# Softmax-factored linear attention into a multiplicative FFN on one core: batch 1's v cast by ScalarE, out evictions in block order, queues listed anew

## The chip, the cores and the metric

One core of a Trainium2 chip runs the kernel. The core has five engines that run side by side, each through its own queue of instructions in the order in which they were emitted: TensorE (PE, with its weight loads PEld), VectorE (DVE), ScalarE (ACT), GpSimd (POOL) and SyncE (SP). 16 DMA engines move data. SP and GpSimd issue the DMAs of this kernel. The metric is the time of one execution on the device in microseconds (us).

## The reference

```python
# q, k, v: (8, 8, 576, 64); moe_w1, moe_w2: (512, 1024); moe_w3: (1024, 1024); moe_w_out: (1024, 512)
q_s = softmax(q, axis=-1)                 # over the head's 64 columns
k_s = softmax(k, axis=2)                  # over the 576 tokens
kv  = einsum('bhsd,bhse->bhde', k_s, v)
attn = einsum('bhsd,bhde->bhse', q_s, kv)
x = attn.transpose(0, 2, 1, 3).reshape(4608, 512)
a = x @ w1
b = x @ w2
out = (a * b @ w3) @ w_out
```

Inputs and output are float32.

## The kernel before

**Folding.** w3 and w_out come right after one another, so the kernel multiplies them once: W3O = w3 @ w_out (1024 x 512, float16). For each of the eight blocks of rows ft: w3t.ft transposes w3's rows on TensorE, w3T.ft copies the result to SBUF, pf.ft.0 and pf.ft.1 multiply by the two halves of w_out (loads wo.0 and wo.1), W3O.ft evicts.

**Attention, for each batch b.** k.b, q.b, v.b load the inputs (batch 0 and 1 of q in two parts). kmx, cba, cbx, cb form a bound of k's columns; ksub.b.hp subtracts it, kexp.b.hp takes the exponential, for two pairs of heads hp. kv.b multiplies by v and sums over the tokens. The denominator of k's softmax is needed too: v lies in a tile with a column of ones beside its 64 columns, which vc.b.hp fills by a cast from float32; then kv.b's 72 matmuls have 65 columns and give the sums as well. For the first VCASTS batches the load itself casts v to float16 into another buffer, without a column of ones; there kv.b has 72 matmuls of 64 columns (L548) and 36 of one column (L558). kve.b and kv2.b divide. On the other side qmx, qsub, qexp, qsm, qeps, qrc, qn form q's softmax in two parts (part 0: 1024 columns, part 1: 1280). It is transposed either by TensorE (qt, then a copy qT) or by a transposing DMA (qd, on SP). xm.b.0 and xm.b.1 multiply transposed q by kv2, xs evicts them to x; xt and xts do the same for the last 64 tokens of a batch, which all batches collect into one tail chunk.

**FFN, for each chunk c (0 to 7 the batches' first 512 tokens, 8 the tail).** up.1.c.sub.u and up.0.c.sub.u multiply x by blocks of w2 and w1; bs evicts the first product, ab multiplies the second by it; down.c.tb multiplies the 128-row block tb by W3O, os.c.tb evicts it, st.c.tb stores it. Weights w1 and w2 load in four parts by columns; up.*.0.*.u needs part u in chunk 0.

**Order.** Nothing is scheduled by the framework (manual_schedule). All steps stand in one list, ORDER, by their names with dots; Plan.run emits them in that order, so each engine's queue is the list cut down to its own steps. PICKS names the engine of the steps that have a choice. LOADS is the order of the loads on GpSimd's queue, at most eight in flight: the n-th waits for the landing of the (n-8)-th. HW and LATE are the loads on SP's queue, the first of LATE (q.2) waiting for the last part of w1 (w1.3). Plan.run also checks that the list respects each ring of buffers: PSUM banks "pab" (4, for up, w3t and the later xt), "po" (2, for down, pf and the later xm.b.1), "att" (2, for kv, qt, xm), and SBUF rings for evicted blocks ("osb", 4, and others). For the first 580 steps of the list (LINKED), each VectorE or GpSimd step marked with "port" (the subtractions, qn, the tree of kmx and some more) waits for the marked step ahead of it in the list when that is on the other engine.

```python
            n = HH // 2 if name in APART else dst.shape[1]
...
        dst = vcast[i] if n == "v" and VCAST[i] else inbuf[n][i % 2]
...
            if not VCAST[b]:
                A(("vc", b, hp), {"POOL": (1.15, True), "ACT": (1.15, False)}, 0,
                  lambda eng, hp=hp: vc(hp, eng), [("v", b)] + [("kv", b - 2)] * old)
```

A line of the profile that starts with L324 is the helper copy (casts and copies of bs, os, vc, w3T, qT), L328 and L330 the helper scale (W3O, xs, xts), L405 a load.

Of the kernel before, what the change touches and what calls it, by code (L numbers as in the profile page):

```python
# [77 lines left out]
q.0.0 qmx.0.0 q.0.1 qmx.0.1 qsub.0.1 qexp.0.1 w3.4 wo.0 ident wo.1 qsub.0.0 w3.0 k.0 w3.2 w3.3 w3.5  # L78
w3t.4 w3t.5 w3T.5 pf.5.0 qsm.0.1 q.1.0 v.0 w3T.4 pf.5.1 qexp.0.0 qeps.0.1 qrc.0.1 qsm.0.0 w3.1 w3t.0
k.1 qn.0.1 qeps.0.0 pf.4.0 qrc.0.0 pf.4.1 qt.0.16 W3O.5 qn.0.0 w3T.0 qT.0.16 W3O.4 qt.0.8 pf.0.0  # L80
qt.0.0 w3t.2 w3T.2 w2.0 pf.0.1 w3t.3 w3T.3 kmx.0.0 cba.0 W3O.0 qT.0.8 cbx.0 pf.2.0 qT.0.0 pf.2.1
w1.0 w1.1 pf.3.0 w3t.7 w2.1 W3O.2 w3T.7 pf.3.1 w3t.6 pf.7.0 pf.7.1 w1.2 cb.0 ksub.0.1 kexp.0.1
ksub.0.0 kexp.0.0 kv.0 kve.0 w2.2 w3T.6 W3O.3 qmx.1.0 W3O.7 k.2 qsub.1.0 w3t.1 pf.6.0 w3T.1 kv2.0
xm.0.0 xs.0.0.0 xs.0.0.1 pf.1.0 pf.1.1 w2.3 xm.0.1 kmx.1.0 cba.1 pf.6.1 xs.0.1.1 xs.0.1.0 qexp.1.0
w1.3 v.1 q.1.1 q.2 cbx.1 qsm.1.0 up.1.0.0.0 xt.0 bs.0.0.0 up.0.0.0.0 up.1.0.1.0 up.0.0.1.0 ab.0.0.0
cb.1 qeps.1.0 ksub.1.1 ksub.1.0 bs.0.1.0 up.1.0.0.1 bs.0.0.1 ab.0.1.0 up.0.0.0.1 up.1.0.1.1
up.0.0.1.1 ab.0.0.1 bs.0.1.1 up.1.0.0.2 up.0.0.0.2 up.1.0.1.2 ab.0.1.1 up.0.0.1.2 W3O.1 kexp.1.1
qrc.1.0 xts.0.0 bs.0.0.2 up.1.0.0.3 ab.0.0.2 bs.0.1.2 kmx.2.0 kexp.1.0 cba.2 qn.1.0 bs.0.0.3 W3O.6
xts.0.1 up.0.0.0.3 up.1.0.1.3 ab.0.0.3 down.0.0 ab.0.1.2 cbx.2 cb.2 ksub.2.0 bs.0.1.3 kv.1
up.0.0.1.3 qmx.1.1 ksub.2.1 ab.0.1.3 kve.1 os.0.0 qsub.1.1 kv2.1 down.0.1 down.0.2 qd.1.0 kexp.2.0  # L90
kexp.2.1 os.0.1 qmx.2.1 xm.1.0 xs.1.0.1 xs.1.0.0 qmx.2.0 qsub.2.1 down.0.3 qexp.1.1 os.0.2
up.1.1.0.0 qsm.1.1 up.0.1.0.0 up.1.1.0.1 qexp.2.1 qeps.1.1 bs.1.0.0 qsm.2.1 qrc.1.1 qsub.2.0 v.2
vc.2.0 vc.2.1 ab.1.0.0 qexp.2.0 qsm.2.0 qn.1.1 qeps.2.1 bs.1.0.1 up.0.1.0.1 up.1.1.0.2 ab.1.0.1
qrc.2.1 st.0.0 k.3 q.3 kv.2 bs.1.0.2 qeps.2.0 kve.2 up.0.1.0.2 up.1.1.0.3 up.0.1.0.3 os.0.3 kv2.2
qt.1.16 qt.1.8 bs.1.0.3 ab.1.0.2 ab.1.0.3 qrc.2.0 down.1.0 qn.2.1 qT.1.8 qT.1.16 xm.1.1 xs.1.1.0
st.0.1 st.0.2 v.3 down.1.1 qn.2.0 qmx.3.0 qmx.3.1 qsub.3.0 qd.2.1 qd.2.0 kmx.3.0 xs.1.1.1 xt.1
up.1.1.1.0 up.0.1.1.0 xts.1.0 qexp.3.0 xts.1.1 os.1.1 bs.1.1.0 up.1.1.1.1 up.0.1.1.1 ab.1.1.0
bs.1.1.1 xm.2.0 cba.3 up.1.1.1.2 up.0.1.1.2 ab.1.1.1 qsm.3.0 xs.2.0.1 xs.2.0.0 xm.2.1 bs.1.1.2
up.1.1.1.3 up.0.1.1.3 cbx.3 xs.2.1.1 xs.2.1.0 up.1.2.0.0 ab.1.1.2 qsub.3.1 up.0.2.0.0 cb.3 bs.1.1.3
qeps.3.0 qrc.3.0 ab.1.1.3 st.0.3 k.4 qexp.3.1 bs.2.0.0 up.1.2.0.1 up.0.2.0.1 up.1.2.0.2 q.4 v.4 q.5  # L100
os.1.0 ksub.3.1 ksub.3.0 qsm.3.1 down.1.2 down.1.3 vc.3.1 qeps.3.1 vc.3.0 kmx.4.1 qrc.3.1 ab.2.0.0
kmx.4.0 cba.4 kexp.3.1 kexp.3.0 bs.2.0.1 up.0.2.0.2 os.1.3 ab.2.0.1 bs.2.0.2 qn.3.0 qmx.4.1 qn.3.1
ab.2.0.2 os.1.2 cbx.4 cb.4 up.1.2.0.3 kv.3 kve.3 kv2.3 bs.2.0.3 up.0.2.0.3 ab.2.0.3 up.1.2.0.4
up.0.2.0.4 xt.2 qd.3.0 qd.3.1 xts.2.1 up.1.2.0.5 up.0.2.0.5 xts.2.0 vc.4.0 qsub.4.1 bs.2.0.4 qmx.4.0
ab.2.0.4 bs.2.0.5 ab.2.0.5 xm.3.1 xm.3.0 xs.3.1.0 up.1.2.0.6 up.0.2.0.6 up.1.2.0.7 xs.3.0.1 xs.3.0.0
bs.2.0.6 xs.3.1.1 qmx.5.1 ksub.4.0 qsub.4.0 vc.4.1 ab.2.0.6 qexp.4.1 qexp.4.0 up.0.2.0.7 up.1.3.0.0
bs.2.0.7 up.0.3.0.0 up.1.3.0.1 qsm.4.1 ab.2.0.7 qeps.4.1 qsm.4.0 qrc.4.1 qsub.5.1 up.0.3.0.1
ksub.4.1 bs.3.0.0 qn.4.1 kexp.4.0 qeps.4.0 up.1.3.0.2 bs.3.0.1 down.2.0 qexp.5.1 kexp.4.1 ab.3.0.0
st.1.1 qrc.4.0 k.5 st.1.2 kmx.5.1 qmx.5.0 st.1.0 v.5 vc.5.0 st.1.3 q.6 ab.3.0.1 up.0.3.0.2 down.2.1
os.2.0 qd.4.1 qn.4.0 qd.4.0 kv.4 xt.3 bs.3.0.2 qsub.5.0 kmx.5.0 kve.4 os.2.1 cba.5 ab.3.0.2 down.2.2  # L110
down.2.3 vc.5.1 qexp.5.0 os.2.2 up.1.3.0.3 xts.3.1 os.2.3 xts.3.0 kv2.4 xm.4.0 qsm.5.1 bs.3.0.3
qeps.5.1 xm.4.1 xt.4 qsm.5.0 up.0.3.0.3 cbx.5 cb.5 qeps.5.0 xts.4.1 xts.4.0 qmx.6.0 ab.3.0.3
xs.4.0.0 xs.4.0.1 xs.4.1.1 xs.4.1.0 k.6 qrc.5.0 up.1.3.0.4 bs.3.0.4 up.0.3.0.4 up.1.3.0.5 up.0.3.0.5
ab.3.0.4 up.1.3.0.6 up.0.3.0.6 bs.3.0.5 ab.3.0.5 bs.3.0.6 up.1.3.0.7 up.0.3.0.7 up.1.4.0.0 qrc.5.1
ksub.5.1 ksub.5.0 q.7 st.2.2 kmx.6.1 kexp.5.1 kexp.5.0 ab.3.0.6 kv.5 up.0.4.0.0 st.2.1 qsub.6.0
qmx.7.0 qn.5.1 qn.5.0 bs.3.0.7 ab.3.0.7 bs.4.0.0 up.1.4.0.1 kve.5 ab.4.0.0 kmx.6.0 st.2.3 st.2.0 v.6
up.0.4.0.1 down.3.0 down.3.1 bs.4.0.1 qd.5.1 qd.5.0 os.3.1 os.3.0 v.7 down.3.2 qmx.6.1 kv2.5 cba.6
ab.4.0.1 up.1.4.0.2 os.3.2 xm.5.0 xm.5.1 xt.5 bs.4.0.2 cbx.6 qexp.6.0 xts.5.0 xts.5.1 up.0.4.0.2
up.1.4.0.3 up.0.4.0.3 up.1.4.0.4 qsub.7.0 qsub.6.1 vc.6.1 vc.6.0 qmx.7.1 xs.5.0.0 bs.4.0.3 xs.5.1.1
qexp.6.1 ab.4.0.2 qsm.6.0 ab.4.0.3 cb.6 bs.4.0.4 xs.5.1.0 up.0.4.0.4 ab.4.0.4 xs.5.0.1 up.1.4.0.5  # L120
up.0.4.0.5 bs.4.0.5 ab.4.0.5 up.1.4.0.6 up.0.4.0.6 bs.4.0.6 ab.4.0.6 up.1.4.0.7 up.0.4.0.7 bs.4.0.7
up.1.5.0.0 up.0.5.0.0 ksub.6.1 qeps.6.0 kexp.6.1 down.3.3 qsub.7.1 ab.4.0.7 up.1.5.0.1 up.0.5.0.1
ksub.6.0 vc.7.0 kexp.6.0 qexp.7.0 bs.5.0.0 qsm.6.1 qeps.6.1 qrc.6.0 qn.6.0 ab.5.0.0 qrc.6.1 qexp.7.1
bs.5.0.1 st.3.0 k.7 st.3.1 qn.6.1 vc.7.1 qsm.7.0 os.3.3 qsm.7.1 up.1.5.0.2 kv.6 up.0.5.0.2 kve.6
bs.5.0.2 down.4.0 down.4.1 os.4.0 qeps.7.0 down.4.2 up.1.5.0.3 ab.5.0.1 kv2.6 qd.6.0 qd.6.1 st.3.2
xm.6.0 ab.5.0.2 kmx.7.1 os.4.1 os.4.2 xm.6.1 xt.6 bs.5.0.3 st.3.3 qeps.7.1 qrc.7.1 qn.7.1 qd.7.1
st.4.0 up.0.5.0.3 xts.6.0 xts.6.1 ab.5.0.3 xs.6.0.0 xs.6.1.1 xs.6.0.1 kmx.7.0 up.1.5.0.4 up.0.5.0.4
up.1.5.0.5 bs.5.0.4 ab.5.0.4 bs.5.0.5 up.0.5.0.5 up.1.5.0.6 up.0.5.0.6 up.1.5.0.7 cba.7 ab.5.0.5
up.0.5.0.7 xs.6.1.0 cbx.7 bs.5.0.6 cb.7 ksub.7.1 ab.5.0.6 bs.5.0.7 ab.5.0.7 up.1.6.0.0 up.0.6.0.0
# [794 lines left out]
```

## Time and profile before

| | |
|---|---|
| runs (median of 3; lowest, highest) | 240.86 us; 240.09, 241.2 |
| the profiled execution | 240.74 us |
| its span, first to last instruction | 239.0 us |
| TensorE, VectorE, ScalarE, GpSimd busy | 229.9, 179.8, 118.0, 111.4 us |
| moved by DMA | 45.93 MB, mean 192 GB/s |

How to read it: the page gives busy time by engine; then 40 equal slices of the span with each engine's busy share in tenths; then the DMA queues; the chain of work that ended last; the costliest groups of instructions; and the DMA issues. A group's row reads: line, engine, operation, what it writes <- what it reads, partitions x elements and types, xcount | busy us, mean ns of one | idle time of the engine before them and what ended it. In a timeline the row is start, duration, engine, line, operation, and in brackets the idle time ahead of it and its releaser. Matmuls overlap, so the cost of a step of TensorE is read from start to start.

### The profile page before, as it was taken

How to read it: one execution, taken by the hardware profiler on the slowest of the kernel's cores; microseconds unless marked ns; L12 is line 12 of the kernel's file. 1: busy time of each engine (PE TensorE's matmuls, PEld its weight loads, DVE VectorE, ACT ScalarE, POOL GpSimd, SP SyncE). 2: the span in 40 equal slices, each digit the busy share in tenths (PEclk: the TensorE clock that was granted, in tenths of full speed). 3: DMA queues.
4: the chain of work that ended last, by engine and by line, in shares of the span. 5: the costliest groups of instructions: out<-in, count | busy, mean ns of one | idle time of the engine just before them, and what ended most of it. 6: DMA issues, size and time to landing. Idle time of an engine off the chain costs nothing.

```text
span 239.0 us, 4936 instructions
## 1 busy us (share of the span) xinstructions
PE 229.9 (96%) x1971; PEld 120.1 (50%) x1971; DVE 179.8 (75%) x273; ACT 118.0 (49%) x222; POOL 111.4 (47%) x74
## 2 busy tenths in 40 slices
...
PEclk9999999999999999999999999999999999999999
DMA  6999999999999989999979702626063000150813
GB/s 210 217 304 252 295 210 300 245 270 329 393 290 295 397 225 231 381 278 263 346 234 235 310 3 44 145 48 139 0 134 88 4 0 0 44 134 21 199 44 132
DMA packets 38998, 45.93 MB, mean 192 GB/s; under 512 B 17088, under 2 KB 23488, under 8 KB 38976
## 3 DMA queue, kind: packets, MB, share of 16 engines
...
q8 instruction: 15, 0.25, 0.4%
...
## 4 chain that ended last, share of the span: by engine, by line
PE 76%; DMA 13%; POOL 4%; DVE 3%; ACT 1%; issue 1%; POOLq 0%; ACTq 0%
PE pab L783 47%; PE po L805 21%; DMA v<-in_v_dram 7%; DMA wosb<-in_moe_w_out_dram 4%; PE po L820 3%; DMA qT<-en 3%; POOL k L523 2%; PE pkv L548 2%; PE xm L666 1%; DVE kmx L497 1%; POOL q L586 1%; POOL en L618 1%; DVE kmx L498 1%; PE po L666 1%; ACT osb L324 0%
## 5 line engine op out<-in xcount | busy, mean ns | idle before, releaser
L798 DVE TENSOR_TENSOR ab<-pab,bsb 128x512 f16<-128x512 f32 x72 | 48.9, 682 | 25.9 <-PE pab L783 14.5
L783 PE MATMUL pab<-x,w1sb 128*128 128x512 f16 (+1 forms) x320 | 66.0, 337 | 0.0
L783 PE MATMUL pab<-x,w2sb 128*128 128x512 f16 (+1 forms) x320 | 65.9, 337 | 0.0
L805 PE MATMUL po<-W3O,ab 128*128 128x512 f16 x256 | 58.9, 379 | 0.7 <-ACT osb L324 0.7
L783 PEld LDWEIGHTS <-w2sb 128*128 128x128 f16 x352 | 34.0, 98 | 28.3 <-issue 0.9
L783 PEld LDWEIGHTS <-w1sb 128*128 128x128 f16 x352 | 33.7, 98 | 26.7
L324 ACT CAST bsb<-pab 128x512 f16<-128x512 f32 x46 | 26.8, 585 | 35.0 <-PE pab L783 29.0
L523 POOL TENSOR_TENSOR k<-k,cb 128x1152 f32<-128x1152 f32 x13 | 34.0, 2629 | 19.2 <-DVE cb L519 17.0
L805 PEld LDWEIGHTS <-ab 128*128 128x128 f16 x256 | 24.7, 98 | 29.9 <-issue 1.4
L324 ACT COPY osb<-po 128x512 f32<-128x512 f32 (+1 forms) x28 | 16.0, 571 | 41.6 <-PE po L805 31.9
L618 POOL TENSOR_TENSOR en<-eq,qr 128x1280 f16<-128x1280 f16 (+1 forms) x12 | 25.8, 2165 | 12.8 <-DMA out_dram<-osb 6.1
L586 POOL TENSOR_TENSOR q<-q,qm 128x1280 f32<-128x1280 f32 (+1 forms) x13 | 27.8, 2149 | 6.5 <-DMA qT<-en 4.5
L581 DVE TENSOR_REDUCE qm<-q 128x16 f32<-128x1024 f32 (+1 forms) x16 | 21.4, 1341 | 3.7 <-DMA q<-in_q_dram 3.7
L324 DVE CAST bsb<-pab 128x512 f16<-128x512 f32 x26 | 17.7, 685 | 6.2 <-PE pab L783 5.9
L599 DVE TENSOR_REDUCE qr<-eq 128x20 f32<-128x1280 f16 (+1 forms) x16 | 21.4, 1340 | 1.0 <-ACT eq L594 0.7
L531 ACT ACTIVATE ek<-k 128x1152 f16<-128x1152 f32 x16 | 18.3, 1161 | 5.3 <-POOL k L523 4.9
L594 ACT ACTIVATE eq<-q 128x1280 f16<-128x1280 f32 (+1 forms) x16 | 18.3, 1160 | 2.1 <-DVE q L586 1.7
L488 DVE TENSOR_REDUCE km<-k 128x128 f32<-128x1152 f32 x8 | 17.1, 2132 | 0.0
L456 PE MATMUL po<-wosb,w3T 128*128 128x512 f16 x64 | 15.6, 379 | 1.4 <-DMA wosb<-in_moe_w_out_dram 1.3
L324 DVE COPY osb<-po 128x512 f32<-128x512 f32 x9 | 6.2, 687 | 7.4 <-PE po L805 7.4
L328 ACT ACTIVATE x<-xm 128x512 f16<-128x512 f32 x16 | 9.1, 596 | 4.6 <-PE xm L666 4.5
L456 PEld LDWEIGHTS <-w3T 128*128 128x128 f16 x64 | 5.7, 98 | 7.6 <-issue 1.8
...
## 6 DMA issues: line engine op xcount, KB each, us to landing
...
q<-in_q_dram SPq DMA_DIRECT2D x5, 1152.0 KB, 8.6
v<-in_v_dram SPq DMA_DIRECT2D x5, 1152.0 KB, 8.2
k<-in_k_dram SPq DMA_DIRECT2D x4, 1152.0 KB, 6.8
k<-in_k_dram POOLq DMA_DIRECT2D x3, 1152.0 KB, 13.6
v<-in_v_dram POOLq DMA_DIRECT2D x2, 576.0 KB, 15.0
q<-in_q_dram SPq DMA_DIRECT2D x2, 576.0 KB, 7.5
v<-in_v_dram SPq DMA_DIRECT2D x2, 576.0 KB, 5.2
```

Source lines behind the costliest of these rows:

```text
L324: return [(nc.scalar.copy if eng == "ACT" else engine[eng].tensor_copy)(out=out, in_=in_)]
L456: nc.tensor.matmul(st["pf", ft], lhsT=st["w3T", ft][:, gt, :], rhs=wosb[:, gt, :], start=(gt == 0), stop=(gt == N_FT - 1))
L523: return [engine[eng].tensor_tensor(out=kb[:, two(hp), :, :], in0=kb[:, two(hp), :, :], in1=st["cb", b][:, two(hp), None, :].broadcast_to( ...
L531: nc.scalar.activation(out=st["ek", b][:, hp, :, :].rearrange("p j (i d) -> p i j d", i=2), in_=kb[:, two(hp), :, :], func=AF.Exp)
L581: dve.tensor_reduce(out=st["qm", b][:, :, j], in_=qb[:, :, j, :], axis=AX.X, op=ALU.max)
L586: return [engine[eng].tensor_tensor(out=qb[:, :, j, :], in0=qb[:, :, j, :], in1=st["qm", b][:, :, j, None].broadcast_to([P, HH, n, D]), op ...
L594: nc.scalar.activation(out=st["eq", b, p], in_=qb[:, :, j, :], func=AF.Exp)
L599: dve.tensor_reduce(out=st["qr", b][:, :, slice(*PARTS[p])], in_=st["eq", b, p], axis=AX.X, op=ALU.add)
L618: return [engine[eng].tensor_tensor(out=st["en", b][:, j, :, :].rearrange("p j h d -> p h j d"), in0=st["eq", b, p], in1=st["qr", b][:, :, ...
L783: nc.tensor.matmul(st["p", one, c, sub, u][:, a * (t1 - t0):(a + 1) * (t1 - t0)], lhsT=w[:, ct, fb * P:(fb + 1) * P], rhs=x()[:, ct, t0:t1 ...
L798: dve.tensor_tensor(out=st["ab", c][:, nf * u:nf * u + nf, t0:t1], in0=cut(st["p", 0, c, sub, u]), in1=cut(st["bsb", c, sub, u]), op=ALU.mult)
L805: nc.tensor.matmul(st["po", c, tb], lhsT=st["ab", c][:, ft, tb * P:(tb + 1) * P], rhs=W3O[:, ft, :], start=(ft == 0), stop=(ft == N_FT - 1))
```

## The change

VCASTS goes from 2 to 1, so batch 1's v loads as float32 and is cast beside the column of ones, by vc.1.0 and vc.1.1, which PICKS gives to ScalarE; kv.1 becomes 72 matmuls of 65 columns. Each os step must stand in the list after the os step of the block before it. ORDER, PICKS, HW, LOADS and LATE are listed anew; the steps are otherwise the same.

```diff
-    VCASTS = 2
+    VCASTS = 1
...
+        old_os = [("os", c - 1, 3)] if c else []
...
                     A(("os", c, tb), moves(C), 0, lambda eng, tb=tb: os(tb, eng), [("down", c, tb)],
-                      lead=EVICT, gives=[("down", c, tb)], takes="osb")
+                      lead=EVICT, gives=[("down", c, tb)], takes="osb", after=old_os)
+                    old_os = [("os", c, tb)]
...
 HW = [
-    ("q", 0, 0), ("q", 0, 1),
+    ("q", 0, 1), ("q", 0, 0),
 ]
...
 LOADS = [
-    ("w3", 4), ("wo", 0), ("wo", 1), ("w3", 0), ("k", 0), ("w3", 2), ("w3", 3), ("w3", 5), ("q",
-    1, 0), ("v", 0), ("w3", 1), ("k", 1), ("w2", 0), ("w1", 0), ("w1", 1), ("w2", 1), ("w1", 2),
-    ("w2", 2), ("k", 2), ("w2", 3), ("w1", 3), ("v", 1), ("q", 1, 1),
+    ("w3", 4), ("wo", 0), ("wo", 1), ("w3", 2), ("k", 0), ("w3", 0), ("w3", 3), ("w3", 5),
+    ("w3", 1), ("v", 0), ("k", 1), ("w2", 0), ("q", 1, 0), ("w1", 0), ("w2", 1), ("w1", 1),
+    ("w1", 2), ("w2", 2), ("k", 2), ("w2", 3), ("w1", 3), ("v", 1), ("q", 1, 1),
 ]
...
 LATE = [
-    ("q", 2), ("v", 2), ("k", 3), ("q", 3), ("v", 3), ("k", 4), ("q", 4), ("v", 4), ("q", 5),
-    ("k", 5), ("v", 5), ("q", 6), ("k", 6), ("q", 7), ("v", 6), ("v", 7), ("k", 7),
+    ("q", 2), ("v", 2), ("k", 3), ("q", 3), ("k", 4), ("v", 3), ("q", 4), ("v", 4), ("q", 5),
+    ("k", 5), ("v", 5), ("q", 6), ("k", 6), ("v", 7), ("q", 7), ("v", 6), ("k", 7),
 ]
```

The parts of the new ORDER around the steps that the prediction names (the start, kv.1 and xm.1.0, qsub.3, os.3):

```diff
+q.0.1 qmx.0.1 qsub.0.1 qexp.0.1 q.0.0 ident w3.4 w3t.5 qmx.0.0 qsm.0.1 wo.0 wo.1 w3.2 k.0 w3.0 w3.3
+w3.5 w3t.4 w3T.5 w3.1 w3T.4 qeps.0.1 qsub.0.0 qrc.0.1 qexp.0.0 qn.0.1 v.0 pf.5.0 pf.4.0 pf.5.1 w3t.2
...
+ksub.1.1 bs.0.1.1 ab.0.0.1 up.0.0.0.2 up.1.0.1.2 qeps.1.0 xts.0.1 qrc.1.0 qn.1.0 bs.0.0.2 ab.0.1.1
+ab.0.0.2 kmx.2.0 cba.2 bs.0.1.2 kexp.1.1 up.0.0.1.2 up.1.0.0.3 up.0.0.0.3 up.1.0.1.3 bs.0.0.3 W3O.6
+qd.1.0 cbx.2 ab.0.0.3 ksub.1.0 down.0.0 ab.0.1.2 cb.2 vc.1.1 kexp.1.0 vc.1.0 os.0.0 ksub.2.1
+up.0.0.1.3 down.0.1 ksub.2.0 qmx.1.1 qsub.1.1 kv.1 bs.0.1.3 os.0.1 kve.1 kexp.2.1 kexp.2.0 ab.0.1.3
+down.0.2 kv2.1 xm.1.0 down.0.3 xs.1.0.1 xs.1.0.0 up.1.1.0.0 up.0.1.0.0 up.1.1.0.1 qmx.2.1 qmx.2.0
...
+qsub.3.1 qsub.3.0 qexp.3.0 up.1.2.0.0 up.0.2.0.0 bs.1.1.3 kmx.4.1 ab.1.1.3 qexp.3.1 bs.2.0.0 qsm.3.0
...
+st.2.1 qd.5.0 st.2.2 bs.4.0.0 kmx.6.0 kmx.6.1 os.3.0 up.1.4.0.1 down.3.2 os.3.1 qmx.6.0 kve.5 kv2.5
```

In the list before, batch 1 stood so: `... down.0.0 up.0.0.1.3` with kv.1 right after down.0.0 on TensorE, ksub.1.1, ksub.1.0 and then qn.1.0 on GpSimd; os.3.1 stood ahead of os.3.0, with os.3.1 on ScalarE and os.3.0 on VectorE, and `down.3.0 down.3.1 down.3.2` followed one another on TensorE; qsub.3.0 was on VectorE.

141 lines of the change are left out of this document (66 added, 75 removed), and 96 rows, old and new, of the table PICKS.

## The prediction

> **What bounds the kernel now.** I read the page first, then the waits of TensorE, the chain of waits, and last the timelines around the two places where TensorE stands still late.
>
> ```profile
> PE 229.9 (96%) x1971; PEld 120.1 (50%) x1971; DVE 179.8 (75%) x273; ACT 118.0 (49%) x222; POOL 111.4 (47%) x74
> PEclk9999999999999999999999999999999999999999
> DMA  6999999999999989999979702626063000150813
> PE po L351 <- DVE zero L346: 1.5, 1, 1.5
> PE po L456 <- DMA wosb<-in_moe_w_out_dram: 1.3, 1, 1.3
> PE w3t L444 <- DMA w<-in_moe_w_dram: 1.0, 2, 0.8
> PE pkv L548 <- DMA v<-in_v_dram: 0.9, 1, 0.9
> PE po L805 <- ACT osb L324: 0.7, 1, 0.7
> PE xm L666 <- DMA qT<-en: 0.5, 1, 0.5
> ```
>
> TensorE is busy 96% of the span, its granted clock in the top tenth throughout; the last six rows are all of its waits (us in total, times, longest). Four of them lie in the first 30 us. After that it stops twice: 0.5 us for the transposed q of batch 1 and 0.7 us for an eviction. From 56 us on the end is therefore set by the sum of the matmuls, which the change does not alter, plus what stalls. Ahead of 56 us another resource binds: the DMA engines are full in nearly every slice up to about 125 us. The chain of waits (start, us, what) has the transfer that ends this part, and the end of the span:
>
> ```profile
> 49.41 6.21 DMA qT<-en
> ...
> 228.95 6.95 PE po L820 x40
> ...
> 235.96 0.37 ACT osb L324
> ```
>
> So there are two stretches: up to xm.1.0, which starts right after that transfer at 55.7, the DMA engines set the time; from there to 235.9 TensorE does, and then one eviction and its store. Profiled time 240.74 = span 239.0 + 1.74 around it; the median of the runs is 240.86, 0.12 more.
>
> **The change part by part.**
>
> *Batch 1's v with a column of ones.* It removes the 36 one-column matmuls of kv.1, widens its 72 matmuls from 64 to 65 columns, and adds vc.1.0 and vc.1.1, both ScalarE.
>
> ```profile
> 45.95 1.04 PE L783 MATMUL pab<-x,w1sb 128*128 128x256 f16 x8
> 46.83 1.04 PE L783 MATMUL pab<-x,w2sb 128*128 128x256 f16 x8
> 47.70 1.89 PE L805 MATMUL po<-W3O,ab 128*128 128x512 f16 x8
> 49.52 0.78 PE L548 MATMUL pkv<-v,ek 64*64 64x64 f16 x72
> 50.23 0.60 PE L558 MATMUL pkv<-ones,ek 64*128 64x1 f16 x36
> 50.77 1.05 PE L783 MATMUL pab<-x,w1sb 128*128 128x256 f16 x8
> 55.75 0.41 PE L666 MATMUL xm<-qT,kv 64*64 64x256 f16 x8 [0.48 <-DMA qT<-en]
> L324 ACT CAST v<-v 128x1152 f16<-128x1152 f32 x5 | 5.7, 1143 | 0.0
> L531 ACT ACTIVATE ek<-k 128x1152 f16<-128x1152 f32 x16 | 18.3, 1161 | 5.3 <-POOL k L523 4.9 <-DVE k L523 0.2
> ```
>
> By the starts, kv.1 costs 50.23-49.52 = 0.71 and its ones 50.77-50.23 = 0.54 us. Removing the ones is worth 0.54, if TensorE is not waiting anyway; the sixty-fifth column costs under 0.02 (72 matmuls in 0.71, one column in 65). The casts cost ScalarE 2 x 1.14.
>
> *Loads listed anew.* q.1.0 goes from ninth of GpSimd's queue to thirteenth, w3.1 from eleventh to ninth; v.0 stays tenth. Ahead of w1.0 the same bytes stand in both, and ahead of w1.3 too.
>
> ```profile
> 33.69 0.74 POOL L405 DMA_DIRECT2D w1sb<-in_moe_w_dram  x1 [0.40 <-DMA w2sb<-in_moe_w_dram]
> 35.01 0.74 POOL L405 DMA_DIRECT2D v<-in_v_dram  x1 [0.58 <-DMA w1sb<-in_moe_w_dram]
> w1sb<-in_moe_w_dram POOLq DMA_DIRECT2D x1, 256.0 KB, 11.9
> v<-in_v_dram POOLq DMA_DIRECT2D x1, 576.0 KB, 13.4
> k<-in_k_dram POOLq DMA_DIRECT2D x1, 1152.0 KB, 13.2
> ```
>
> w1.3 lands at 33.69+11.9 = 45.6, v.1 at 35.01+13.4 = 48.4. v.1 now lands as 1152 KB of float32 where 576 KB of float16 landed; k.2, of that form, takes 13.2 from issue to landing, so I take no difference (bounds: 0 to +1.5, if the queue went by bytes written). The identity now stands ahead of all loads on GpSimd, which starts them about 0.5 us later. I cost that at nothing: the two loads of q.0 are then on their way on SP, and the wait before xm.1.0 absorbs what is left; without this cover it is 0.5.
>
> *What TensorE does up to xm.1.0.* pf.4.0 now stands between pf.5.0 and pf.5.1, in the 1.3 us wait for the second half of w_out; v.0 comes earlier; w3t.1 moves ahead of kv.0. All this brings TensorE forward, until up.0.0.0.3 needs w1.3 at 45.6 (it started at 45.95 before). From there in the new order: two quarters of up 1.74, down.0.0 1.73 (four such blocks take 6.95 at the end of the chain), one more up 0.87, down.0.1 1.73, so kv.1 is reached at 51.7. On ScalarE vc.1.1, kexp.1.0 and vc.1.0 follow v.1: 48.4 + 2 x 1.14 + 1.16 = 51.9, a wait of 0.2. Queued behind them are bs.0.1.3, os.0.1 and kve.1; ab.0.1.3 waits for the first, down.0.2 in its last matmuls for that, and both are covered by kv.1 and down.0.2's first six. Then kv.1 0.71 and down.0.2 1.73: TensorE stands at xm.1.0 at 54.3, one us sooner than before.
>
> *What xm.1.0 waits for.* qn.1.0 goes between ksub.1.1 and ksub.1.0 and is some 4 us earlier. But qd.1.0 stands behind q.2 on SP:
>
> ```profile
> 45.63 0.37 SPq L405 DMA_DIRECT2D q<-in_q_dram  x1
> 49.41 1.34 SPq L641 DMA_TRANSPOSE qT<-en  x1
> q<-in_q_dram SPq DMA_DIRECT2D x1, 1152.0 KB, 9.1
> qT<-en SPq DMA_TRANSPOSE x1, 6.2
> ```
>
> q.2 waits for w1.3 in both kernels and lands at 45.63+9.1 = 54.7; the transpose, issued 3.8 us after it, lands at 55.6, 0.9 behind. I read that as the transpose following q.2 through the engines, so issuing it at 46.4 brings little: xm.1.0 at 55.65, a gain of 0.1. Bounds: 0, if nothing moves; and if it takes its 6.2 us from its new issue (52.6), TensorE goes on at 54.3. Then ScalarE decides next: behind vc.1.0 at 51.9 stand bs, os, kve, two kexp and two xs (0.59, 0.59, 0.41, 1.16, 1.16, two of 0.6, less 0.1 of overlap each), and up.1.1.0.0, at 57.83 before, starts at 56.7. That bound is -1.1. I take -0.1, by the row of the transpose itself. So the 0.54 of the ones, the moved transposes and the filled wait become a wait of 1.3 us before xm.1.0 in place of 0.5.
>
> The Trainium skill (DMA: Bandwidth & Descriptors, Queues, rings and completion order) says that an engine consumes the descriptors of one ring in their order, and that one issuing sequencer owns one ring on each DMA engine. By that rule the early issue buys nothing, and the sum stays at -0.1 here; by the row's 6.2 us counted from issue it would be -1.1. The trace agrees with the rule, with 0.9 us between the landings against 3.8 between the issues.
>
> *Evictions in the order of their blocks.* The one later stall:
>
> ```profile
> 125.94 0.69 DVE L324 COPY osb<-po 128x512 f32<-128x512 f32 x1 [0.63 <-PE po L805]
> 127.66 0.59 ACT L324 COPY osb<-po 128x512 f32<-128x512 f32 x1 [3.73 <-PE po L805]
> 128.30 1.89 PE L805 MATMUL po<-W3O,ab 128*128 128x512 f16 x8 [0.68 <-ACT osb L324]
> ```
>
> os.3.0 is done at 126.6, a whole us before down.3.2 could start, and yet down.3.2 waits for os.3.1: the old list names os.3.1 first, and I read the row so that the bank is handed on in the order of the list. In the new list os.3.0 is named first, on ScalarE, down.3.2 stands ahead of os.3.1, and up.1.4.0.1 lies between down.3.1 and down.3.2. So 0.68 goes. Bounds: 0 to -0.68; I take all.
>
> *The rest of the lists.* k.4 goes ahead of v.3, v.7 ahead of q.7; some twenty evictions and subtractions change engine. The same matmuls follow, so only new stalls count.
>
> ```profile
> 60.00:80.00 20.00, 20.00 (x241) 14.26 (x240) 18.89 (x32) 15.90 (x35) 13.01 (x7) 1.00 1.06 334
> 80.00:100.00 20.00, 20.00 (x174) 9.01 (x173) 19.44 (x26) 15.65 (x30) 19.24 (x11) 1.00 0.97 290
> ```
>
> The columns are TensorE, its weight loads, VectorE, ScalarE, GpSimd. VectorE is nearly full here. Summing its list by the durations of the groups, I find no more work ahead of any chunk's first up in the new list than in the old (0.3 to 5 us less). Walking the queues from row to row up to chunk 3, the narrowest inputs of TensorE are ready 0.3 to 0.5 us ahead. I take 0 (bounds 0 to +2, the rival below). The tail is cut as before, ScalarE evicts last: 0.
>
> Sum: 240.74 - 0.1 - 0.68 + 0 = 239.96, against the median 240.1; I say 240.0.
>
> **The rivals.**
>
> *The transpose lands early.* For: its issue moves up by 3 us and its input is ready. Against: it landed 0.9 behind q.2. Then -1.1 - 0.68: 240.74 - 1.8 = 239.0 (238.6 to 239.5).
>
> *The order brings nothing.* The eviction wait stays, or small stalls eat it. Against: the row shows the older eviction long done. Time: 240.74 - 0.1 = 240.6 (240.4 to 241.0).
>
> *A new stall, slower than before.* qsub.3.0 moves from VectorE to GpSimd, behind qsub.3.1; on ScalarE bs.1.1.3 and bs.2.0.0 are queued behind qexp.3.0 and qexp.3.1, which wait for them; and TensorE needs the banks that these two free.
>
> ```profile
> 73.32 2.34 POOL L586 TENSOR_TENSOR q<-q,qm 128x1280 f32<-128x1280 f32 x1 [4.51 <-DMA qT<-en]
> L586 POOL TENSOR_TENSOR q<-q,qm 128x1024 f32<-128x1024 f32 x6 | 11.5, 1919 | 0.0
> L594 ACT ACTIVATE eq<-q 128x1024 f16<-128x1024 f32 x8 | 8.4, 1054 | 0.0
> ```
>
> At the old start of qsub.3.1 this gives 73.3 + 2.3 + 1.9 + 1.05 + 0.6 = 79.2 for bs.1.1.3, and up.1.2.0.1 needs its bank at 79.9. VectorE no longer has qsub.3.0 (1.2 us) ahead of kmx.3.0, on which qsub.3.1 waits, so the margin is 0.7 + 1.2 = 1.9 us. It decides from there, at one us for each us. Were the chain 4 to 5 us late, as the 4.5 us that GpSimd idles before this row shows to be possible, it costs 2 to 3: 240.74 - 0.8 + 2.5 = 242.4 (241.2 to 243).
>
> **How the numbers follow.** Forecast (239.6 to 240.4) 0.45; transpose early 0.25; nothing gained 0.12; new stall 0.18. About 0.5%, 1.2 us, is what a measurement tells from no change here: faster is under 239.66, slower over 242.06. Faster takes the early transpose and a quarter of the forecast: 0.37. Slower takes most of the new stall: 0.16. The rest, 0.47, is the same. The range leaves out the outer half of both outer cases: 238.7 to 242.2.
>
> **What would show it.** TensorE reaches kv.1 near 51.7, and its wait at xm.1.0 for the transpose of q grows to about 1.3 us, with xm.1.0 starting near 55.6; if it starts at 54.3 the first rival holds. The rows of L558 halve to 36. No wait of the down matmuls on an eviction of 0.7 us is left among TensorE's waits. From up.1.1.0.0 to the last down the timeline is shorter by 0.7. I am wrong if TensorE's waits after 56 us sum to more than 1 us, above all on pab banks between 75 and 85 us, or if v.1 lands after 49.5 and kv.1 waits for the casts.

## The result and the profile after

| | before | after |
|---|---|---|
| median (lowest to highest), 6 runs each | 240.87 us (240.09 to 241.2) | 239.42 us (239.21 to 239.62) |
| the profiled execution | 240.74 us | 239.21 us |
| its span | 239.0 us | 237.4 us |

The ratio of after to before is 0.9943, 95% interval 0.9929 to 0.9957: 1.45 us shorter, 0.6%. The forecast was 240.0, the first rival 239.0 (238.6 to 239.5); the time lies between them, within the rival's range. What the rival forecast, transposes that land early, is what happened, though not for the reason that the prediction gave it.

The page of the changed kernel, TensorE's row and the clock that it was granted (lines of the changed kernel stand one further down: L325 is the helper copy, L784 up, L806 down, L667 xm):

```profile
PE 230.1 (97%) x1935; PEld 119.5 (50%) x1935; DVE 180.3 (76%) x277; ACT 121.7 (51%) x221; POOL 110.0 (46%) x73
PEclk9999999999999999999999999999999999999999
```

All waits of TensorE (us in total, times, longest):

```profile
PE po L352 <- DVE zero L347: 1.6, 1, 1.6
PE w3t L445 <- DMA w<-in_moe_w_dram: 1.2, 3, 0.8
PE po L457 <- DMA wosb<-in_moe_w_out_dram: 0.5, 1, 0.5
PE xm L667 <- DMA qT<-en: 0.5, 1, 0.5
PE pab L784 <- DVE kmx L499: 0.4, 1, 0.4
```

TensorE's work is the same 230 us. The 0.7 us for an eviction is gone. A wait of 0.5 us for transposed q stands there as before, but it is not the same one. TensorE's timeline (start, us, what, and in brackets the idle time ahead of it):

```profile
45.79 1.05 PE L784 MATMUL pab<-x,w1sb 128*128 128x256 f16 x8 [0.36 <-DVE kmx L499]
...
50.15 1.89 PE L806 MATMUL po<-W3O,ab 128*128 128x512 f16 x8
52.05 0.80 PE L549 MATMUL pkv<-v,ek 64*64 64x65 f16 x72
52.78 1.90 PE L806 MATMUL po<-W3O,ab 128*128 128x512 f16 x8
54.62 0.41 PE L667 MATMUL xm<-qT,kv 64*64 64x256 f16 x8
...
71.87 1.04 PE L784 MATMUL pab<-x,w1sb 128*128 128x256 f16 x8
73.37 0.41 PE L667 MATMUL xm<-qT,kv 64*64 64x512 f16 x4 [0.46 <-DMA qT<-en]
...
121.57 3.63 PE L806 MATMUL po<-W3O,ab 128*128 128x512 f16 x16
125.04 1.03 PE L784 MATMUL pab<-x,w2sb 128*128 128x512 f16 x4
125.90 1.89 PE L806 MATMUL po<-W3O,ab 128*128 128x512 f16 x8
```

The wait at 45.79 is that for w1.3, which landed at 45.75; run 12 has the same wait with that load as its releaser. xm.1.0 starts at 54.62 without a wait, 1.13 us sooner than before. The new wait of 0.46 us is at xm.2.0, batch 2. Before, xm.2.0 had none:

```profile
73.00 1.04 PE L783 MATMUL pab<-x,w1sb 128*128 128x256 f16 x8
73.97 0.41 PE L666 MATMUL xm<-qT,kv 64*64 64x512 f16 x4
```

So 0.60 of the 1.13 us is left at xm.2.0. down.3.2 (125.90) starts right behind up.1.4.0.1: the wait of 0.68 is gone. Read from start to start it was worth 0.82: before, down.3.0 and down.3.1 took 128.30 - 124.01 = 4.29 us until down.3.2 started, here they take 125.04 - 121.57 = 3.47. The last 0.11 of the 1.53 us by which the last matmuls come sooner are spread over smaller steps and were not followed.

The chain of waits (start, us, what) has the transposes of batch 2 where it had those of batch 1:

```profile
66.24 2.09 DVE qm L582 x2
68.35 4.89 DMA qT<-en
```

What made xm.1.0 earlier is seen in the DMA view of the changed kernel for the transfers issued between 45.2 and 52 us (KB each, us from issue to landing):

```profile
q<-in_q_dram SPq DMA_DIRECT2D x1, 1152.0 KB, 7.7
qT<-en SPq DMA_TRANSPOSE x1, 8.2
```

q.2 was issued at 45.81 and landed at 53.53, 7.7 us, where it took 9.1 before; the transposes (one transfer, issued by qd.1.0), issued at 46.23, landed at 54.39, 0.86 behind it (0.93 before). The DMA view of the stretch from 51 to 55 us shows the difference. Before (engines' busy share in 40 slices of 0.1 us, GB/s, then packets, MB and share of 16 engines by queue):

```profile
DMA  9999999992372122224199980000000000003999
...
q1 hardware_dynamic: 1151, 0.46, 112.2%
q8 instruction: 1, 0.02, 3.8%
```

and after:

```profile
DMA  9999999999392333362811499999999599999998
...
q1 hardware_dynamic: 1402, 1.02, 117.4%
```

Before, one packet of 16 KB of instructions lies in this stretch. Its share, 3.8% of 16 engines over 4 us, is 2.4 us; by its record it ran from 51.4 to 53.9, and other packets of the kind took 0.9 to 1.3. The digits need care: a packet's whole time is booked in the slice in which it starts, so a zero says that hardly a packet starts, not that the engines are free. From 53.4 to 54.6 us that is so. The view of 53.1 to 53.3 us, before and then after, shows why:

```profile
q1 hardware_dynamic: 98, 0.03, 847.0%
...
q1 hardware_dynamic: 44, 0.01, 30.0%
```

Before, packets worth 8.5 times these 0.2 us start there: sixteen packets of the transposes, 256 bytes each, stand for 1.5 us, to 54.7. After, no packet of instructions is there (it came at 56.5), and from 53.3 us on packets start at the full rate again. The experiments had to tell whether this packet is the cause.

### The profile page after: what moved, and what is told of

It reads as the page before. It is cut to its first block, busy times and chain, and to the rows that moved or that the text cites. A ratio compares the mean times of both kernels' runs of the same rounds, so it can differ in the third digit from the quotient of the medians.

```text
span 237.4 us, 4860 instructions
## 1 busy us (share of the span) xinstructions
PE 230.1 (97%) x1935; PEld 119.5 (50%) x1935; DVE 180.3 (76%) x277; ACT 121.7 (51%) x221; POOL 110.0 (46%) x73
## 4 chain that ended last, share of the span: by engine, by line
PE 81%; DMA 8%; DVE 5%; POOL 4%; issue 1%; ACT 0%; POOLq 0%; ACTq 0%
PE pab L784 46%; PE po L806 22%; DMA w<-in_moe_w_dram 6%; PE po L457 4%; PE po L821 3%; PE pkv L549 2%; DMA qT<-en 2%; PE xm L667 1%; DVE qm L582 1%; POOL k L524 1%; PE w3t L445 1%; POOL en L619 1%; POOL w L406 1%; DVE ab L799 1%; DVE kmx L498 1%
## 5 line engine op out<-in xcount | busy, mean ns | idle before, releaser
L784 PE MATMUL pab<-x,w1sb 128*128 128x512 f16 (+1 forms) x320 | 65.9, 337 | 0.4 <-DVE kmx L499 0.4
L784 PE MATMUL pab<-x,w2sb 128*128 128x512 f16 (+1 forms) x320 | 66.0, 337 | 0.0
L799 DVE TENSOR_TENSOR ab<-pab,bsb 128x512 f16<-128x512 f32 x72 | 48.6, 682 | 20.2 <-PE pab L784 13.6
L806 PE MATMUL po<-W3O,ab 128*128 128x512 f16 x256 | 58.9, 379 | 0.0
L784 PEld LDWEIGHTS <-w1sb 128*128 128x128 f16 x352 | 34.2, 98 | 28.5 <-DMA w1sb<-in_moe_w_dram 0.6
L784 PEld LDWEIGHTS <-w2sb 128*128 128x128 f16 x352 | 33.5, 98 | 27.5 <-issue 0.7
L325 ACT CAST bsb<-pab 128x512 f16<-128x512 f32 x46 | 26.8, 582 | 35.8 <-PE pab L784 34.6
L524 POOL TENSOR_TENSOR k<-k,cb 128x1152 f32<-128x1152 f32 x12 | 31.4, 2628 | 16.4 <-issue 5.1
L806 PEld LDWEIGHTS <-ab 128*128 128x128 f16 x256 | 24.5, 98 | 28.5 <-issue 0.4
L587 POOL TENSOR_TENSOR q<-q,qm 128x1024 f32<-128x1024 f32 (+1 forms) x14 | 29.5, 2125 | 13.1 <-DVE rc L573 5.4
L325 ACT COPY osb<-po 128x512 f32<-128x512 f32 (+1 forms) x25 | 14.3, 571 | 40.3 <-PE po L806 26.8
L619 POOL TENSOR_TENSOR en<-eq,qr 128x1024 f16<-128x1024 f16 (+1 forms) x13 | 27.2, 2106 | 10.5 <-DVE qr L612 10.4
L582 DVE TENSOR_REDUCE qm<-q 128x20 f32<-128x1280 f32 (+1 forms) x16 | 21.2, 1340 | 3.6 <-DMA q<-in_q_dram 3.6
L325 DVE CAST bsb<-pab 128x512 f16<-128x512 f32 x26 | 17.6, 677 | 6.8 <-PE pab L784 6.3
L325 DVE COPY osb<-po 128x512 f32<-128x512 f32 x12 | 8.3, 688 | 9.1 <-PE po L806 7.9
L329 ACT ACTIVATE x<-xm 128x512 f16<-128x512 f32 x18 | 10.3, 597 | 6.4 <-PE xm L667 6.2
L325 ACT CAST v<-v 128x1152 f16<-128x1152 f32 x9 | 10.3, 1148 | 0.3 <-DMA v<-in_v_dram 0.3
## 6 DMA issues: line engine op xcount, KB each, us to landing
v<-in_v_dram POOLq DMA_DIRECT2D x1, 1152.0 KB, 13.9
```

What stands on the lines that cost most here:

```text
L325: return [(nc.scalar.copy if eng == "ACT" else engine[eng].tensor_copy)(out=out, in_=in_)]
L524: return [engine[eng].tensor_tensor(out=kb[:, two(hp), :, :], in0=kb[:, two(hp), :, :], in1=st["cb", b][:, two(hp), None, :].broadcast_to( ...
L582: dve.tensor_reduce(out=st["qm", b][:, :, j], in_=qb[:, :, j, :], axis=AX.X, op=ALU.max)
L587: return [engine[eng].tensor_tensor(out=qb[:, :, j, :], in0=qb[:, :, j, :], in1=st["qm", b][:, :, j, None].broadcast_to([P, HH, n, D]), op ...
L619: return [engine[eng].tensor_tensor(out=st["en", b][:, j, :, :].rearrange("p j h d -> p h j d"), in0=st["eq", b, p], in1=st["qr", b][:, :, ...
L784: nc.tensor.matmul(st["p", one, c, sub, u][:, a * (t1 - t0):(a + 1) * (t1 - t0)], lhsT=w[:, ct, fb * P:(fb + 1) * P], rhs=x()[:, ct, t0:t1 ...
```

## The experiments

Each run is compared with the kernel before on the same chip; "landing" is the end of a transfer by its record, a packet's time is that of its record. Of a row of ORDER or PICKS the diffs show the part that changes.

**1. The transposes issued late.**

```diff
-qd.1.0 cbx.2 ab.0.0.3 ksub.1.0 down.0.0
+cbx.2 ab.0.0.3 ksub.1.0 qd.1.0 down.0.0
...
-            nc.sync.dma_start_transpose(out=qTt()[:, n0:n1, :], in_=blocks(st["en", b], n0, n1))
+            d = nc.sync.dma_start_transpose(out=qTt()[:, n0:n1, :], in_=blocks(st["en", b], n0, n1))
+            if b == 1:
+                link(d, st["late"])
```

st["late"] is the last ksub that was emitted, here ksub.1.0.

> The changed kernel, but the transposing transfer of batch 1 (qd.1.0) waits for ksub.1.0, which ended at 49.4 us in the profile of the changed kernel, so that it is issued at the 49.4 us of before. Theory A (the earlier issue made q.2 and the transpose behind it land earlier): q.2 lands near 54.7 again instead of 53.5, the transpose near 55.6, xm.1.0 starts near 55.7 instead of 54.62, the new wait of 0.46 us at xm.2.0 is swallowed, so the time is 1.1 - 0.46 = 0.6 us longer, near 240.0. Theory B (the loads ahead of q.2 were done sooner, and q.2 with them): q.2 lands near 53.5 all the same, the transpose under one us behind it or at most at 49.4 + 6.2 = 55.6 if its time counts from issue; xm.1.0 at 54.7 to 55.0, and the time is unchanged within 0.1, 239.4.

Measured: 239.72 us, ratio 0.9956 (0.994 to 0.9971), which overlaps the changed kernel's. In its trace w1.3 landed 0.6 us later than in the changed kernel's, though the two are alike up to there (by so much do single traces differ), and everything up to xm.1.0 is later by as much; the DMA view gives, for the same stretch,

```profile
q<-in_q_dram SPq DMA_DIRECT2D x1, 1152.0 KB, 7.7
qT<-en SPq DMA_TRANSPOSE x1, 5.4
```

q.2 takes 7.7 us again and the transposes, issued 3.2 us after it, land 0.88 behind it. The time of issue is worth nothing, as the prediction had it; theory A fell. That q.2 itself lands sooner was not explained by this run.

**2 and 3. The order of the evictions, and what stands between the downs.**

```diff
# 2
-os.3.0 up.1.4.0.1 down.3.2 os.3.1 qmx.6.0
+os.3.1 os.3.0 down.3.2 up.1.4.0.1 qmx.6.0
-    "os_3_0": "ACT"
+    "os_3_0": "DVE"
-                      lead=EVICT, gives=[("down", c, tb)], takes="osb", after=old_os)
+                      lead=EVICT, gives=[("down", c, tb)], takes="osb")
# 3
-os.3.0 up.1.4.0.1 down.3.2 os.3.1 qmx.6.0
+os.3.0 down.3.2 up.1.4.0.1 os.3.1 qmx.6.0
```

> The changed kernel, with os.3.1, os.3.0, down.3.2 and up.1.4.0.1 in the order and on the engines of before. Theory A (the order of the list hands the bank on): down.3.2 waits for os.3.1 again, 0.6 to 0.7 us, and the time is 0.7 us longer, near 240.1. Theory B (the wait had another cause, or is given back later): no such wait, 239.4.

> The changed kernel, with up.1.4.0.1 behind down.3.2 instead of between down.3.1 and down.3.2; the evictions stay in the order of their blocks. Theory A (the order of the evictions alone removes the wait): down.3.2 follows down.3.1 without a wait and the time is unchanged, 239.4. Theory B (the 0.87 us of up.1.4.0.1 in between covers the eviction of os.3.1): down.3.2 waits 0.6 to 0.7 us and the time is near 240.1.

Measured: 241.53 us, ratio 1.0034 (1.0021 to 1.0047), and 240.77 us, ratio 1.0001 (0.9989 to 1.0014). Both are slower than expected. TensorE's timeline of run 2:

```profile
121.24 3.63 PE L806 MATMUL po<-W3O,ab 128*128 128x512 f16 x16
125.59 1.89 PE L806 MATMUL po<-W3O,ab 128*128 128x512 f16 x8 [0.72 <-ACT osb L325]
...
130.66 0.40 PE L667 MATMUL po<-qT,kv 64*64 64x512 f16 x2 [0.91 <-ACT osb L325]
```

The first wait is the old one, back with the old order; run 3 hasn't got it, and the two differ by 241.53 - 240.77 = 0.76 us. So the order of the two evictions decides which one down.3.2 waits for, and it is worth 0.7 to 0.9 (0.88 read from start to start over the three downs). os.3.0 changes its engine along with the order; that this has no part in it is argued from the trace of before, where os.3.0 was done a us ahead of need, and not shown by a run. The second wait, 0.91 at xm.5.1, stands in both. ScalarE's timeline of run 3 says why:

```profile
127.60 0.59 ACT L325 CAST bsb<-pab 128x512 f16<-128x512 f32 x1 [1.64 <-PE pab L784]
128.09 1.27 ACT L595 ACTIVATE eq<-q 128x1280 f16<-128x1280 f32 x1
129.26 0.58 ACT L325 COPY osb<-po 128x512 f32<-128x512 f32 x1
```

os.3.2, whose bank xm.5.1 needs, is queued behind bs.4.0.1, and that waits for up.1.4.0.1, which now comes behind down.3.2. In the changed kernel bs.4.0.1 starts at 126.10 and os.3.2 at 127.83, as soon as down.3.2 is done. So the place of up.1.4.0.1 matters after all, for a wait that isn't at down.3.2 but one eviction later. Theory B of run 3 had a cost right, but not its place. Of the 2.1 and 1.35 us by which runs 2 and 3 are longer than the changed kernel, these waits are 1.63 and 0.91; the other 0.4 to 0.5 stay open.

**4. The ones back.**

```diff
-    VCASTS = 1
+    VCASTS = 2
-vc.1.1 kexp.1.0 vc.1.0
+kexp.1.0
```

> The changed kernel, with batch 1's v loaded as float16 and the 36 matmuls against the column of ones in kv.1 again, without vc.1.0 and vc.1.1. Theory A (the removal is hidden): kv.1 takes 0.54 us more but needs no cast, so it starts about 0.1 us sooner; xm.1.0 starts near 55.0 instead of 54.62, and the wait of 0.46 us at xm.2.0 shrinks by as much: time unchanged, 239.3 to 239.6. Theory B (part of the gain is the ones removed): 0.4 to 0.54 us longer, 239.9.

Measured: 239.32 us, ratio 0.994 (0.9928 to 0.9953): no difference to the changed kernel. xm.1.0 starts at 55.01, 0.39 later, and xm.2.0 at 73.23, 0.14 sooner, because qd.2.0 lands at 71.71 instead of 73.23. Theory A holds for the time, and its wait shrank to nothing, but by an earlier landing that the run's expectation had not named (its packet came at 66.8 instead of 71.2). So the run shows the ones and the moved packet together.

**5 to 7. Where the packet of instructions comes.** One of the kernel before with a single step of TensorE moved, one of before and one of after with more matmuls at the start.

```diff
# 5
-bs.0.1.3 kv.1
-up.0.0.1.3 qmx.1.1 ksub.2.1 ab.0.1.3 kve.1 os.0.0 qsub.1.1 kv2.1 down.0.1 down.0.2 qd.1.0
+bs.0.1.3 up.0.0.1.3
+down.0.1 kv.1 qmx.1.1 ksub.2.1 ab.0.1.3 kve.1 os.0.0 qsub.1.1 kv2.1 down.0.2 qd.1.0
# 6 (7: "begin": 14 and range(52))
-    "begin": 17, "pf.5.0": 6,
+    "begin": 12, "pf.5.0": 6,
...
         fill(FILL["begin"])
+        idle = p_o()
+        for i in range(80):
+            nc.tensor.matmul(idle[0:32, 0:1], lhsT=zero[:, 0:32], rhs=zero[:, 0:1], start=True, stop=True)
```

> The kernel before, with one move in TensorE's list: kv.1 behind up.0.0.1.3 and down.0.1, where the changed kernel has it, with its ones matmuls and all else as before. In the trace of before a packet of 16 KB of instructions stands among the DMA packets at 51.4 us, takes 2.4 us (the others of its kind take about 1.0) and overlaps the transposes of batch 1; in the changed kernel it comes at 56.5. Theory C (that packet held one DMA engine's share of q.2 and of the transposes; it is fetched as TensorE runs through kv.1, so the place of kv.1 decides when it comes): the packet comes behind the transposes, q.2 lands near 53.5 and the transpose near 54.4; TensorE itself then sets xm.1.0, near 55.1 instead of 55.75, and the time is 0.6 us shorter, near 240.2. Theory D (q.2's landing follows from the order of the loads): the transpose lands at 55.6, xm.1.0 starts at 55.7, 240.8 unchanged.

> The kernel before, with 80 matmuls of one column (160 instructions with their weight loads) added to the opening fill, which loses 5 of its 17 wide ones so that it still ends before the first weights land. Theory C: the instruction transfers come 160 instructions earlier in TensorE's list, the one of 51.4 us before 50.9; the transpose lands near 54.5, xm.1.0 starts at TensorE's own 55.25 instead of 55.75, and the time is 0.5 us shorter, near 240.3. Theory D: nothing moves, xm.1.0 at 55.7, 240.8.

> The changed kernel, with 52 matmuls of one column (104 instructions with their weight loads) added to the opening fill, which loses 3 of its 17 wide ones. Theory C: the instruction transfer of 56.5 us comes near 51.5, on top of the transposes again; q.2 lands near 54.5 and the transpose near 55.5, xm.1.0 starts up to 1.1 us later (55.0 to 55.7), of which the wait of 0.46 us at xm.2.0 swallows its part: 239.5 to 240.1. Theory D: nothing moves, 239.4.

Measured: 241.36 us, ratio 1.0033 (1.002 to 1.0046); 242.1, 1.0058 (1.0042 to 1.0074); 239.72, 0.9959 (0.9947 to 0.9972). The landings came as theory C has them in runs 5 and 6. In run 5 the packet comes at 56.3, q.2 lands at 53.29 and the transposes, issued at 49.42 as before, at 54.16 instead of 55.61. The DMA view of run 5 from 51 to 55 us has no row of instructions:

```profile
DMA  9999899949382712222289999999939999999999
...
q1 hardware_dynamic: 1355, 1.02, 115.7%
```

In run 6 packets come at 48.6 and 53.8, and the transposes land at 54.45, though issued at 51.05; the packet of 53.8, at the end of their data, cost them nothing that shows. The times did not follow, since TensorE itself was later. In run 5 it reaches xm.1.0 only at 56.27, by a new wait at down.0.2 (the other of the two in the first row is the old one at down.3.2; the rows behind it are of its timeline):

```profile
PE po L805 <- ACT osb L324: 1.6, 2, 1.0
...
54.46 1.89 PE L805 MATMUL po<-W3O,ab 128*128 128x512 f16 x8 [0.97 <-ACT osb L324]
56.27 0.41 PE L666 MATMUL xm<-qT,kv 64*64 64x256 f16 x8
```

os.0.0 is queued on ScalarE behind kve.1, which waits for the moved kv.1, and down.0.2 needs its bank. In run 6 the 80 small matmuls took 2.15 us and the wide ones behind them ran slowly, so that pf.5.0 started 1.6 us later; nothing hid that, and xm.1.0 started at 57.22. In run 7 the packet came at 49.3, not near 51.5: q.2 took 8.1 instead of 7.7 us and was issued 0.6 later, the transposes landed at 55.57 (xm.1.0 at 55.70), and qd.2.0, with its packet gone to 68.2, landed 3.1 us after its issue, without a wait at xm.2.0. So theory C holds for what a packet does to the landings; that the time follows, these three runs do not show, and my date of the packet was off by 2 us in run 7.

**8. k.4 behind the transposes of batch 2.**

```diff
-k.4 qd.2.1 qmx.3.0 qmx.3.1 up.1.1.1.0 qn.2.0 bs.1.1.0 xts.1.1 qd.2.0
+qd.2.1 qmx.3.0 qmx.3.1 up.1.1.1.0 qn.2.0 bs.1.1.0 xts.1.1 qd.2.0 k.4
```

> The changed kernel, with the load k.4 behind the two transposes of batch 2 (qd.2.1, qd.2.0) on SP instead of ahead of them. Theory A (the transposes follow k.4 through the queue): qd.2.0 lands before 72.5 instead of 73.23, the wait of 0.46 us at xm.2.0 goes, and the time is 0.4 to 0.5 us shorter, near 239.0. Theory B (qd.2.0 is late because GpSimd hands it over at 68.3 and it takes 4.9 us from there): the wait stays, 239.4; k.4, issued near 70, lands near 76 and kmx.4.1, at 76.5, is not delayed by more than 0.5 us.

Measured: 240.27 us, ratio 0.9978 (0.9964 to 0.9993). qd.2.0 landed at 73.36, 4.65 us after its issue, with nothing of k.4 ahead of it: theory A fell. The time is 0.85 us longer than the changed kernel's; its profiled span, 237.9, accounts for 0.5 of that. k.4 now lands at 77.23, so that kmx.4.1 waits for it and starts 0.7 us later; whether that makes the 0.5 was not followed, and the rest stays open too.

**9 to 11. The packets moved again.**

```diff
# 9
                 st["p", one, c, sub, u] = p_ab()
+                for i in range(36 if (one, c, sub, u) == (0, 0, 0, 3) else 0):
+                    nc.tensor.matmul(st["p", one, c, sub, u][0:32, 0:1], lhsT=zero[:, 0:32], rhs=zero[:, 0:1], start=True, stop=True)
# 10 (11: "begin": 13)
-    "begin": 17, "pf.5.0": 6,
+    "begin": 17,
```

> The changed kernel, with 36 matmuls of one column (72 instructions with their weight loads) in the wait of 0.5 us that TensorE has for w1.3 ahead of up.0.0.0.3. Their results are overwritten by up.0.0.0.3, and they fill a wait, so by themselves they cost nothing. Theory C (the packet of 16 KB of TensorE's instructions comes when TensorE reaches a fixed place of its list, about 950 instructions in, and holds the transfers that it meets): TensorE is there near 50.1 instead of 52.3, the packet comes near 51.4 on top of q.2's end and the transposes, q.2 lands at 54.5 or later, the transpose near 55.5 instead of 54.39, xm.1.0 starts near 55.6 with a wait of about one us. The later packets come 72 instructions earlier too, the one of 71.2 before 69, so the wait at xm.2.0 goes. Together 1.0 - 0.46 = 0.5 us longer, 239.9. Theory D (the instruction packets hold nothing, landings follow from the loads): transpose at 54.4, xm.1.0 at 54.6, 239.4.

> The changed kernel without the 6 matmuls that fill the wait ahead of pf.5.0 (12 instructions with their weight loads fewer, 0.6 us of TensorE's later pace). Theory C: the packet of 71.2 us comes near 71.9, behind most of the transposes of batch 2; qd.2.0 lands near 72.0 instead of 73.23, the wait of 0.46 us at xm.2.0 shrinks to nothing, and the time is 0.3 to 0.5 us shorter, near 239.0; the packet of 56.5 stays behind the transposes of batch 1. Theory D: qd.2.0 lands at 73.2, the wait stays, 239.4. If TensorE runs slower for want of the fill, pf.5.0 and what follows take longer in both, up to w1.3's landing at 45.75, which covers 0.5 us of it.

> The changed kernel without the 6 matmuls ahead of pf.5.0 and with 13 instead of 17 at the start (20 instructions fewer, one us of TensorE's later pace). Theory C: the packet of 71.2 us comes near 72.2, behind the transposes of batch 2; qd.2.0 lands near 71.6, no wait at xm.2.0, 0.46 us shorter, near 239.0. Theory D: qd.2.0 lands at 73.2, the wait stays, 239.4. In both, if the wait of 2 us that the shorter fill leaves ahead of the first weights slows TensorE down, the first folds take longer, with the 0.5 us ahead of w1.3's landing as cover.

Measured: 240.36 us, ratio 0.9979 (0.9967 to 0.9991); 239.3, 0.9947 (0.9928 to 0.9965); 239.88, 0.9968 (0.9945 to 0.999). Run 9 is the changed kernel with the old wait back. TensorE's waits and its timeline:

```profile
PE xm L667 <- DMA qT<-en: 1.4, 2, 1.2
```

```profile
52.88 0.80 PE L549 MATMUL pkv<-v,ek 64*64 64x65 f16 x72
53.61 1.90 PE L808 MATMUL po<-W3O,ab 128*128 128x512 f16 x8
56.67 0.41 PE L667 MATMUL xm<-qT,kv 64*64 64x256 f16 x8 [1.16 <-DMA qT<-en]
```

and its DMA view from 53 to 57 us:

```profile
DMA  1111102499999999800000001101009866999999
...
q8 instruction: 1, 0.02, 1.8%
```

The packet (1.8% of 16 engines over 4 us, 1.2 us) came at 54.1, behind q.2's end (54.02) and inside the transposes; hardly a packet starts from 54.7 to 56.0, since fifteen that started just before stand for 1.4 to 1.7 us each, and the transposes land 2.5 us behind q.2 instead of 0.9. The packet came later than I had put it, and the 36 matmuls took 1.0 us where 0.5 were free; xm.1.0 is 2.05 us later than in the changed kernel, 1.16 of it by this wait. In runs 10 and 11 the packet did not leave the transposes: it came at 70.5 and 72.7, qd.2.0 took 4.6 and 4.9 us, the wait stayed (0.25 and 0.52). Run 11 also lost pace at the start: its granted clock was 0.64 from 9 to 14 us, where the changed kernel has 1.0. Twelve or twenty instructions fewer don't move a packet predictably.

Taken together, the last transposing transfer of batch 2 (qd.2.0, 256 KB) in all kernels derived from the changed one:

| kernel | packet at | issue to landing |
|---|---|---|
| after; 1; 8; 12 | 71.2; 71.8; 70.8; 71.4, inside | 4.88; 4.90; 4.65; 4.87 us |
| 2; 3; 10; 11 | 70.5; 70.5; 70.5; 72.7, inside | 4.56; 4.46; 4.62; 4.92 us |
| 4; 7; 9 | 66.8; 68.2; 69.1, ahead of it | 3.14; 3.12; 3.17 us |

The DMA view of the changed kernel for 68.05 to 74.9 us:

```profile
q8 instruction: 1, 0.02, 0.8%
...
qT<-en SPq DMA_TRANSPOSE x1, 4.9
```

So a packet inside cost qd.2.0 1.3 to 1.8 us, and the new wait at xm.2.0 has the same cause as the old one at xm.1.0. A landing is complete with the last of sixteen signals, and the trace shows which are late: in the changed kernel fifteen come by 71.64 and the last at 73.23, in run 4 all sixteen from 71.55 to 71.71. Runs 1, 11 and 12 also have one signal 1.6 us behind the rest; in 2, 3, 8 and 10 all sixteen are late together.

In runs 4, 7 and 9 the packet is not off the transposes altogether: it lies inside qd.2.1, the transfer ahead of qd.2.0, which took 3.57, 3.88 and 4.29 us there and 3.42 to 3.96 in the other eight. So there it cost little. From the issue of qd.2.1 to the landing of qd.2.0 these three take 5.0 to 5.3 us, the other eight 6.3 to 6.8. Where in the transfers a packet falls therefore counts; why was not found.

**12. Work put into the wait at xm.2.0.**

```diff
-ab.1.1.0 xm.2.0 xs.2.0.0 bs.1.1.1 xs.2.0.1 cbx.3 ab.1.1.1 cb.3 up.1.1.1.2
+ab.1.1.0 up.1.1.1.2 xm.2.0 xs.2.0.0 bs.1.1.1 xs.2.0.1 cbx.3 ab.1.1.1 cb.3
```

> The changed kernel, with up.1.1.1.2 listed ahead of xm.2.0 instead of behind it, so that TensorE has 0.87 us of work while the transposes of batch 2 land. If the wait at xm.2.0 is all that the late landing costs, xm.2.0 starts without a wait (73.6 us, landing at 73.23), up.1.2.0.0 starts 0.46 us sooner, and the time is 0.4 to 0.5 us shorter, near 239.0. Rival: the evictions of xm.2.0 (xs.2.0.0, xs.2.0.1) come 0.2 us later on their engines and push bs.1.1.1 and ab.1.1.1, so that a later up waits for its bank and part of it is given back: 239.2 to 239.5.

Measured: 239.25 us, ratio 0.9936 (0.9913 to 0.9959). No wait at xm.2.0 is left in its trace, and up.1.2.0.0 starts 10.25 us after xm.1.1 where the changed kernel takes 10.78; but 0.27 us are given back at up.0.2.0.3, whose bank comes later. The interval holds the changed kernel's ratio: no gain that this measurement can tell.

## Why the prediction was right, and where it was not

**The ones.** Right in size: worth 0.52 on TensorE (kv.1 took 50.77 - 49.52 = 1.25 with them, and now 52.78 - 52.05 = 0.73). That they are worth nothing in the time is right too, though run 4 shows it only with a moved packet: there the 0.39 us that xm.1.0 lost came back because batch 2's transposes landed early. What hides the ones in the changed kernel is the landing of batch 2's transposes, not, as I had it, that of batch 1's.

**The loads.** Right within 0.3 us: w1.3 landed at 45.75 (45.6 predicted) and v.1 at 48.7 (48.4), though v.1 took 13.9 us from issue to landing instead of 13.4. In the ten kernels that load it as float32 it took 13.5 to 14.5, in the four with float16 13.4 to 13.7; so doubling the bytes written cost a few tenths of a us at most on the whole.

**TensorE up to xm.1.0.** Right: kv.1 started at 52.05 after a short wait for vc.1.0 (predicted 51.9), and TensorE was at xm.1.0 at 54.6 (predicted 54.3; 0.15 of the difference is kv.1's later start, 0.13 that kv.1 and down.0.2 took 2.57 us instead of 2.44).

**What xm.1.0 waits for.** This is the step that failed. The prediction took q.2's landing at 54.7 for both kernels and set the transposes 0.9 behind it, a gain of 0.1. The second half is right: 0.86 to 1.02 us behind q.2 in every trace that has both records but run 9's, at issues from 45.9 to 51.05; and the transposes do queue behind q.2, for their first packet starts at 50.96 before and at 51.12 after, each time as the first of q.2's closing writes ends, whatever their issue. The first half is wrong: the 9.1 us of q.2 in the profile of before were not its own. Without a packet of instructions ahead of its landing it takes 7.6 to 7.9 us (after and runs 1, 2, 4, 5 and 8 to 12). And the packet records say that q.2's data were not late at all: the last of these closing writes, sixteen of 4 bytes, ended 7.0 us after the issue before and 7.1 after. But of the sixteen signals of its landing three came at 54.7, 1.45 us behind the others, just when the sixteen standing packets of the transposes ended. So the transposes did not land late in the wake of q.2, as the step had it: they were under way from 50.96 on, the packet held them, and the last signals of q.2 with them. The place of kv.1 moved that packet out of the way: run 5 does it in the kernel before with that move alone, run 9 puts a packet back into the changed kernel and xm.1.0 waits 1.16 us again. Run 4 excludes the ones themselves, since with them the packet stays at 56.4. The gain at xm.1.0 was 1.13 instead of 0.1, all of the bound that the step had named. That bound came out right by another limit: it had ScalarE set up.1.1.0.0 at 56.7 (its terms add up to 56.3), but TensorE ran from xm.1.0 without a wait to up.1.1.0.0 at 56.70.

The Trainium skill (Runtime: NRT & Kernel Launch, Instruction fetch mechanics) says that a sequencer refills its engine's instructions through its own DMA queue in blocks of 16 KiB, 256 instructions, at a mostly hidden cost. The trace agrees with the block (16 KB each, 15 of them for 2 x 1971 instructions of TensorE and its weight loads, 263 per block; 16 in run 6, with 150 instructions more). The cost was not hidden here where a block met a transposing transfer on which TensorE waits: 1.16 us at xm.1.0 in run 9. The row of instruction packets on the page of before does not say where they fall; the DMA view of a narrow stretch does.

**The evictions.** Right in cause, and nearly in size: 0.68 predicted; 0.82 from start to start in the changed kernel, 0.72 as a wait in run 2 and 0.76 as time between runs 2 and 3. I named up.1.4.0.1 between the downs without saying what it covers; it keeps os.3.2 from being late, 0.91 us (run 3).

**The rest of the lists.** I took 0, with bounds 0 to +2. It was +0.46, at xm.2.0, a place that I had not listed: my walk through the queues used before's duration of the transposes, and theirs is not fixed. The lists differ by more than I had counted, too: 89 steps change their engine, not some twenty. The stall that I had as the slow rival did not come: GpSimd did both parts of qsub.3 from 71.7 to 75.9, three us ahead of up.1.2.0.1 at 79.4.

**The sum.** -0.1 - 0.68 + 0 = -0.78 against -1.13 - 0.82 + 0.53 - 0.11 = -1.53: above all two errors of 1.0 and 0.5 us, of opposite sign and one cause. That they half cancel is luck. The time, 0.6 us under the forecast, lay within the range because it took in the bound of that step; it lies under 239.66, the prediction's line for faster, to which it gave 0.37, against 0.47 for the same. From up.1.1.0.0 to the last down the timeline is 0.40 us shorter, not 0.7, for the new wait lies there.
